# Attention over a K/V cache on one core: V transfers moved to ScalarE's DMA queue, transfers of 512 KB, no limit on bytes outstanding

## The chip, the cores and the metric

One core of a Trainium2 chip. The metric is device time in microseconds (us) of one execution. The kernel before takes 941.17 us (median of 2 runs, 939.9 to 942.44).

## The reference

Two independent blocks, A and B, do the same thing; their outputs are put side by side.

```python
# x: 16 x 64 x 640; k_cache, v_cache: 16 x 32 x 512 x 128; wq: 640 x 4096; wo: 4096 x 640; all bf16
q = (x @ wq).reshape(B, Sq, H, Dh).transpose(0, 2, 1, 3)
scores = einsum("bhqd,bhkd->bhqk", q, k_cache) * Dh ** -0.5
p = softmax(scores)
o = einsum("bhqk,bhkd->bhqd", p, v_cache)
out = o.transpose(0, 2, 1, 3).reshape(B, Sq, H * Dh) @ wo
```

K and V of both blocks are 268 MB, and each byte is used once. With the weights the kernel reads 294.7 MB. There is much to stream, and nearly as much to compute.

## The kernel before

The kernel is a software pipeline that is planned in Python. One *step* is two heads of two batches; there are 256 steps. In each step TensorE (PE) transposes K (KX, 32 small transposes), transposes the softmax rows (TR, 16), projects Q (QP, 10 matmuls), multiplies by V (PV, 16), projects the output (OP, 4) and makes scores (SM, 4). Each matmul instruction also has a weight load, so a step is about 165 PE instructions. ScalarE (ACT) computes exp and copies o; VectorE (DVE) copies transposes out of PSUM; GpSimd normalizes.

K and V lie in rings. A slot holds `G` heads of two batches and is filled by two transfers, one per batch. All loads are issued by SyncE (SP), in an order that the plan finds by counting each transfer's time:

```python
class Cfg:
    G = 2               # heads in a slot; a K or V transfer is G * 128 KB
    CAP = 2100 << 10    # the window: bytes of SP's loads that may be outstanding
    NKB = 10            # slots of the K ring
    NVB = 10            # slots of the V ring
    NXN = 2
...
    for c in range(NCHUNK):
        for kind, ring, n_ring, cons, tb in (("LDK", "kn", cfg.NKB, "KX", 2), ("LDV", "v", cfg.NVB, "PV", 2.5)):
            ready = NEG if c < n_ring else MPC * (c - n_ring + 1) - 1 - OFF[cons]
            need = MPC * c - OFF[cons]
            for j in range(2):
                op = Op("sp", kind, (c, j), [], [(ring, c % n_ring, gi) for gi in range(0, G, 2)],
                        ts=(need, -1), aux=(c, j), dur=cfg.DMA_NS[kind] * G / 2.0)
                loads.append((ready, need, tb + 0.001 * j, op))
    pending = sorted(loads, key=lambda e: (e[1], e[2]))
    ...                               # takes the ready load that is needed first
        progs["sp"].append(e[3])
        t_now += e[3].dur / cfg.SLOT_NS
...
    for op in progs["sp"]:            # the window
        window.append(op)
        done = None
        while sum(size[o.kind] for o in window) > cfg.CAP:
            done = window.pop(0)
        if done is not None:
            op.deps.append(done)      # SP waits until this earlier load has landed
...
        def em_LDKV(e, op):           # (cut)
            if op.kind == "LDV":
                src = blocks[blk][2][2 * bp + j, h0:h0 + G].rearrange("g (p t) d -> p g t d", p=128)
                ins = e.dma_start(v_ring[:, c % NVB, j], src)
            else:
                src = ...             # K, likewise
                ins = e.dma_start(kn_ring[:, c % NKB, j], src)
```

Of the kernel before, what the change touches and what calls it, by code (L numbers as in the profile page):

```python
# [19 lines left out]


class Cfg:
    G = 2
    GW = 4
    CAP = 2100 << 10
    HH = 16
    NKB = 10
    NVB = 10
    NX = 3
    NXN = 2  # L30
    NQ = 2
# [24 lines left out]
        act=("EX0", "EX1", "XE0", "OE0", "OVP0", "ST0"),  # L56
# [26 lines left out]
def build_plan(dims, cfg, stable, counts):  # L83
    NBLK, B, H = dims["NBLK"], dims["B"], dims["H"]
    G, GW = cfg.G, cfg.GW
    HH = min(cfg.HH, H)
    assert H % HH == 0 and HH % G == 0 and G % 2 == 0 and cfg.NR % 2 == 0 and B % 2 == 0
    NHALF = H // HH
# [5 lines left out]
    NMAC = NSTEP // 2  # L94
    NCHUNK = NSTEP // G
    HG = HH // GW
    MPG = HH // 2
    MPP = NBP * MPG
    MPC = G // 2
    MPW = GW // 2  # L100
# [10 lines left out]
    def make_op(eng, kind, sub, k, m):  # L111
        ts = (k, STAGE[kind + str(sub)])

        def mk(idx, reads, writes, aux=None, name=None):
            return Op(eng, name or kind, idx, reads, writes, ts=ts, aux=aux)
# [13 lines left out]
        g = g0 + sub  # L129
        c = g0 // G  # L130
        r = g % cfg.NR
        if kind == "KX":
            return mk(m, [("kn", c % cfg.NKB, g0 % G), ("ident",)], [("KT", 0), ("KT", 1)])
        if kind == "KE":
# [21 lines left out]
        if kind == "PV":  # L156
            return mk(m, [("pT", m % cfg.NT, 0), ("pT", m % cfg.NT, 1), ("v", c % cfg.NVB, g0 % G)], [("B",)])
        if kind == "OE":
# [16 lines left out]
    progs = {e: [] for e in ENGINES}  # L175
    lo = -max(max(OFF.values()), cfg.XLEAD)
    for k in range(lo, NMAC):
        for eng, order in cfg.ENGINE_ORDER.items():
            for name in order:
                kind, sub = name[:-1], int(name[-1])  # L180
                op = make_op(eng, kind, sub, k, k + OFF[kind])
# [15 lines left out]
        progs["dve"].append(Op("dve", "CF", -1, [], [("KT", 0), ("flag",)], ts=(NMAC + 8, 4)))  # L197

    loads = []
    NEG = -10 ** 9  # L200
    for ps_ in range(NPASS):
        buf = ps_ % 2
        for j in range(HG):
            m0 = ps_ * MPP + j * MPW
            for kind, name, cons, tb in (("LDWQ", "wq", "QP", 0), ("LDWO", "wo", "OP", 3)):
                ready = NEG if ps_ < 2 else (ps_ - 1) * MPP - MPG + j * MPW + MPW - 1 - OFF[cons]
                need = m0 - OFF[cons]
                op = Op("sp", kind, (ps_, j), [], [(name, buf, j)], ts=(need, -1), aux=(ps_, j),
                        dur=cfg.DMA_NS[kind])
                loads.append((ready, need, tb, op))  # L210
    for grp in range(NGRP):
        need = MPG * grp - cfg.XLEAD
        op = Op("sp", "LDX", grp, [], [("xn", grp % cfg.NXN)], ts=(need, STAGE["KX0"]), aux=grp,
                dur=cfg.DMA_NS["LDX"])
        loads.append((NEG if grp < cfg.NXN else need - MPG * cfg.NXN, need - 1, 1, op))
    for c in range(NCHUNK):
        for kind, ring, n_ring, cons, tb in (("LDK", "kn", cfg.NKB, "KX", 2), ("LDV", "v", cfg.NVB, "PV", 2.5)):
            ready = NEG if c < n_ring else MPC * (c - n_ring + 1) - 1 - OFF[cons]
            need = MPC * c - OFF[cons]
            for j in range(2):  # L220
                op = Op("sp", kind, (c, j), [], [(ring, c % n_ring, gi) for gi in range(0, G, 2)],
                        ts=(need, -1), aux=(c, j), dur=cfg.DMA_NS[kind] * G / 2.0)
                loads.append((ready, need, tb + 0.001 * j, op))
    pending = sorted(loads, key=lambda e: (e[1], e[2]))
    t_now = min(e[1] for e in loads) - 4.0
    while pending:
# [59 lines left out]
    for op in progs["sp"]:  # L286
# [4 lines that stand above are left out]
# [57 lines left out]
def mha_kernel(nc, blocks, out, cfg=None):  # L348
# [16 lines left out]
    for stable in (False, True):  # L365
        progs, info = build_plan(dims, cfg, stable, counts)
        prune_waits(progs)
        plans.append((progs, info))
    info = plans[0][1]
    NBP, HH, NHALF, NSTEP = info["NBP"], info["HH"], info["NHALF"], info["NSTEP"]  # L370
    NKB, NVB, NX, NXN, NQ, NKT, NP, NPN, NT, NO, NR = (cfg.NKB, cfg.NVB, cfg.NX, cfg.NXN, cfg.NQ, cfg.NKT, cfg.NP,
                                                       cfg.NPN, cfg.NT, cfg.NO, cfg.NR)
# [10 lines left out]
    with contextlib.ExitStack() as es:  # L383
        block = es.enter_context(nc.Block())

        def sb(name, shape, dt):
            return es.enter_context(nc.sbuf_tensor(name, shape, dt))
# [5 lines left out]
        xn_ring = sb("xn_ring", [128, NXN, D], BF16)  # L393
        kn_ring = sb("kn_ring", [128, NKB, 2, G // 2, 8, DH], BF16)
        v_ring = sb("v_ring", [128, NVB, 2, G, 4, DH], BF16)
        ktp_ring = sb("ktp_ring", [128, NKT, 2, 2, SK], BF16)
# [25 lines left out]
        def kt_ps(hs):  # L422
            return ps[:, KT_BANK + hs, :].bitcast(BF16)
# [7 lines left out]
        def rows(r):  # L431
            return slice(64 * r, 64 * r + 64)

        def row_transpose(e, dst, src, r):
            return e.transpose(dst, src, ident[rows(r), rows(r)], tile_position=(64 * r, 0))  # L435

        def em_KX(e, op):
# [3 lines left out]
            for j in range(2):  # L441
                for t8 in range(8):
                    for hs in PAIR:
                        col = 512 * j + 64 * t8
                        ins.append(row_transpose(e, kt_ps(hs)[:, col:col + 64],
                                                 kn_ring[rows(hs), c % NKB, j, hp, t8, :], hs))
            return ins[0], ins[-1]
# [82 lines left out]
        def em_PV(e, op):  # L530
            m = op.idx
            ins = []
            for sub in range(2):
                g = 2 * m + sub
                c, gi = g // G, g % G
                for j in range(2):
                    for t in range(4):
                        col = sub * 128 + 64 * j
                        ins.append(e.matmul(o_ps[:, col:col + 64], v_ring[:, c % NVB, j, gi, t, :],  # L539
                                            pT_ring[:, m % NT, j, sub, t, :], start=(t == 0), stop=(t == 3)))  # L540
# [103 lines left out]
        def em_LDKV(e, op):  # L644
# [3 lines left out]
# [4 lines that stand above are left out]
                src = blocks[blk][1][2 * bp + j, h0:h0 + G].rearrange("(hp hs) (p t) d -> (hs p) hp t d",  # L652
                                                                              hs=2, t=8)
                ins = e.dma_start(kn_ring[:, c % NKB, j], src)
            return ins, ins
# [110 lines left out]
```

## Time and profile before

| | before |
|---|---|
| time, median | 941.17 us |
| steps done by 60 us | 13 |
| steady step, mean of steps 16 to 240 | 3.60 us |
| undisturbed step (10th percentile) | 3.03 us |
| PE gaps that end just after an instruction fetch | 83, together 86 us |

The profiled run took 947.4 us, 0.8% above the fastest of its two timed runs.

The page of the kernel before: span, PE's busy time and instructions, DMA busy tenths and GB/s in 40 slices, two DMA queues (packets, MB, share of 16 engines), and the chain that ended last, by engine.

```profile
span 945.6 us, 48361 instructions
PE 830.7 (88%) x21153; PEld 592.1 (63%) x21153; DVE 669.3 (71%) x1812; ACT 446.6 (47%) x1329; POOL 416.2 (44%) x518
...
DMA  8999999999999999999999999998999999999930
GB/s 293 320 344 354 346 361 356 354 344 355 332 355 336 324 315 318 310 330 325 323 346 363 354 322 330 314 324 278 334 339 324 352 348 302 332 299 326 303 116 12
...
q1 hardware_dynamic: 236544, 294.72, 93.2%
q8 instruction: 170, 2.79, 1.2%
...
PE 77%; issue 10%; DMA 6%; DVE 5%; ACT 1%; SPq 0%; ACTq 0%; DVEq 0%
```

DMA looks saturated by its busy tenths, but the windows view gives 351 GB/s at 60-300 us, then 329 and 321 in the next two stretches of 300 us, so later there is some room. "issue" is time in which PE waited for nothing that the profile shows, and it is 10% of the chain. Two more views say the same. The waits (engine, line, waited for: us in total, times, longest), first PE's and then those of SP's queue:

```profile
PE ps L435 <- issue: 47.1, 44, 2.7
PE ps L539 <- issue: 23.1, 22, 2.1
PE ps L461 <- issue: 11.3, 12, 1.9
```

```profile
SPq L650 <- PE ps L539: 76.5, 112, 3.1
SPq L654 <- PE ps L435: 71.8, 107, 2.4
```

SP waits for PE to free V (L650) and K (L654) slots, so the rings are mostly full. Data is seldom late: all of PE's waits for DMA sum to 15 us, against 81.5 us in the three lines above. What PE lacks shows in the timeline (start, length, engine, line, operation; in brackets the idle time before):

```profile
305.50 0.68 PE L461 MATMUL ps<-xT_ring,wq_sb 128*128 128x128 bf16 x9
307.42 0.23 PE L461 MATMUL ps<-xT_ring,wq_sb 128*128 128x128 bf16 x1 [1.24 <-issue]
307.49 0.63 PE L539 MATMUL ps<-pT_ring,v_ring 128*128 128x64 bf16 x16
```

PE stops between the ninth and the tenth Q matmul. No semaphore is awaited there; the next *instruction* is missing. The DMA records of the trace (queue q8) hold 170 transfers of 16 KB of instructions. One ran from 304.30 to 306.04, and PE went on at 307.42, 1.4 us after it landed. Nearly every gap like this ends 1.2 to 1.7 us after such a transfer, at places in PE's program 251.4 matmul and weight-load instructions apart. With PE's other instructions that is a block of 256. The Trainium skill ("Runtime: NRT & Kernel Launch", Instruction fetch mechanics) describes it: instructions are refilled in 16 KiB blocks of 256, the next while the current one executes. The trace agrees. The skill also calls the cost "mostly hidden", and with 86 us of gaps here the trace does not.

From the records two quantities can be worked out for every fetch:

- **delay**: from PE's start on the block before (taken as the moment of the request) to the start of the fetch's data. An undisturbed block lasts 4.6 us (251.4 instructions at 165.3 a step and 3.03 us a step). The data takes about 1.0 us and PE restarts 1.4 us later, so by this estimate a delay above about 2.2 us stalls PE.
- **backlog**: bytes issued, at the end of their issue instruction, less bytes whose packets have started.

Before, the mean delay is 2.94 us, and the mean backlog at a request is 0.86 MB. The delay depends on which instruction is taken for the start of the block: a check that counted every PE instruction gave means 0.2 us lower.

The first Q projection of the run, and a stretch by the windows view (stretch and its length, busy time of each engine with instruction counts, PE clock, DMA share, GB/s):

```profile
3.97 0.70 ACT L640 ACTIVATE xT_ring<-ps 128x640 bf16<-128x640 bf16 x1 [1.90 <-PE ps L635]
...
6.24 1.25 PE L461 MATMUL ps<-xT_ring,wq_sb 128*128 128x128 bf16 x10 [2.30 <-DMA wq_sb<-in_A_wq_dram]
```

```profile
100.00:850.00 750.00, 670.72 (x17251) 478.34 (x17248) 542.35 (x1472) 363.55 (x1084) 337.54 (x416) 0.98 0.99 332
```

### The profile page before, as it was taken

The numbers are of one execution on the slowest core, as the hardware profiler recorded it, in microseconds if no ns is written. First come the engines' busy times: TensorE is split into PE (matmuls) and PEld (weight loads), VectorE is DVE, ScalarE is ACT, GpSimd is POOL, SyncE is SP. The second block draws the span as 40 slices with busy tenths as digits, with TensorE's granted clock in tenths as the row PEclk, the third lists the DMA queues.
The fourth block names the chain that finished last, engine by engine and source line by source line (L and its number), as shares of the span: only waits on it lengthen the run. The fifth ranks groups of instructions, "written<-read, shape, count | busy, mean of one in ns | idle before, by whom it ended". The sixth has DMA issues, their size and how long they took to land.

```text
span 945.6 us, 48361 instructions
## 1 busy us (share of the span) xinstructions
PE 830.7 (88%) x21153; PEld 592.1 (63%) x21153; DVE 669.3 (71%) x1812; ACT 446.6 (47%) x1329; POOL 416.2 (44%) x518
## 2 busy tenths in 40 slices
PE   6798889888889999989889999998888889898895
PEld 4466666566566666667566666666556566666663
DVE  4477766777567777768677677776667777777785
ACT  3345444454445544544445455554444445445452
POOL 3244444444345444444445444444444444444442
PEclk9899999999999999999999999999999999999999
DMA  8999999999999999999999999998999999999930
GB/s 293 320 344 354 346 361 356 354 344 355 332 355 336 324 315 318 310 330 325 323 346 363 354 322 330 314 324 278 334 339 324 352 348 302 332 299 326 303 116 12
DMA packets 239066, 300.52 MB, mean 318 GB/s; under 512 B 17664, under 2 KB 173312, under 8 KB 238848
## 3 DMA queue, kind: packets, MB, share of 16 engines
q1 hardware_dynamic: 236544, 294.72, 93.2%
q8 instruction: 170, 2.79, 1.2%
q10 hardware_dynamic: 2304, 2.62, 0.8%
q14 instruction: 48, 0.39, 0.1%
HBM read 294.65 MB, written 2.62 MB: 314 GB/s over the span
## 4 chain that ended last, share of the span: by engine, by line
PE 77%; issue 10%; DMA 6%; DVE 5%; ACT 1%; SPq 0%; ACTq 0%; DVEq 0%
PE ps L435 21%; PE ps L461 16%; PE ps L555 14%; PE ps L474 13%; PE ps L539 12%; DMA v_ring<-in_A_v_cache_dram 3%; DVE ktp_ring L451 2%; DVE pT_ring L526 1%; DMA wq_sb<-in_A_wq_dram 1%; DMA wo_sb<-in_A_wo_dram 1%; PE ps L635 1%; DVE out_sb L568 1%; ACT p_ring L495 1%; DMA kn_ring<-in_A_k_cache_dram 1%; DVE qT_ring L467 0%
## 5 line engine op out<-in xcount | busy, mean ns | idle before, releaser
L510 POOL TENSOR_SCALAR pn_ring<-p_ring,recip 128x512 bf16<-128x512 bf16 x512 | 415.6, 840 | 516.0 <-DVE recip L502 516.0
L451 DVE COPY ktp_ring<-ps 128x1024 bf16<-128x1024 bf16 x512 | 345.6, 682 | 158.3 <-PE ps L435 158.2
L495 ACT ACTIVATE p_ring<-ps 128x512 bf16<-128x512 f32 x512 | 300.5, 593 | 49.0 <-DVE out_sb L568 23.0
L544 ACT ACTIVATE oT_ring<-ps 128x256 bf16<-128x256 f32 x256 | 97.9, 383 | 386.3 <-DVE pT_ring L526 385.4
L526 DVE COPY pT_ring<-ps 128x512 bf16<-128x512 bf16 x512 | 193.3, 419 | 85.5 <-PE ps L539 85.1
L435 PEld LDWEIGHTS ps<-ident,kn_ring 64*128 64x128 bf16 x8192 | 138.1, 96 | 125.7 <-issue 105.3
L461 PE MATMUL ps<-xT_ring,wq_sb 128*128 128x128 bf16 x2560 | 193.5, 223 | 13.6 <-issue 11.3
L555 PE MATMUL ps<-wo_sb,oT_ring 128*128 128x512 bf16 (+1 forms) x1024 | 186.6, 305 | 8.2 <-DMA wo_sb<-in_A_wo_dram 6.2
L539 PE MATMUL ps<-pT_ring,v_ring 128*128 128x64 bf16 x4096 | 169.7, 195 | 23.8 <-issue 23.1
L435 PE MATMUL ps<-ident,kn_ring 64*128 64x64 bf16 x8192 | 170.9, 192 | 17.1 <-issue 14.2
L474 PE MATMUL ps<-ktp_ring,qT_ring 128*64 128x512 bf16 x1024 | 165.3, 399 | 3.1 <-issue 1.6
L461 PEld LDWEIGHTS ps<-xT_ring,wq_sb 128*128 128x128 bf16 x2560 | 147.4, 99 | 30.0 <-issue 14.3
L539 PEld LDWEIGHTS ps<-pT_ring,v_ring 128*128 128x128 bf16 x4096 | 149.0, 99 | 27.0 <-issue 25.3
L435 PE MATMUL ps<-ident,pn_ring 64*128 64x64 bf16 x4096 | 108.1, 191 | 38.5 <-issue 32.9
L467 DVE CAST qT_ring<-ps 128x256 bf16<-128x256 f32 x256 | 108.7, 425 | 16.1 <-PE ps L461 7.5
L435 PEld LDWEIGHTS ps<-ident,pn_ring 64*128 64x128 bf16 x4096 | 80.7, 96 | 41.4 <-issue 37.2
L495 ACT ACTIVATION_READ_ACCUMULATOR p_ring<-ps 128x1 f32 x512 | 102.5, 200 | 0.0
L555 PEld LDWEIGHTS ps<-wo_sb,oT_ring 128*128 128x128 bf16 x1024 | 74.1, 99 | 42.7 <-issue 7.0
L474 PEld LDWEIGHTS ps<-ktp_ring,qT_ring 128*64 128x64 bf16 x1024 | 38.3, 108 | 75.7 <-issue 71.6
L502 DVE RECIPROCAL recip<-sums 128x1 f32<-128x1 f32 x512 | 78.6, 153 | 8.8 <-ACT p_ring L495 8.8
L640 ACT ACTIVATE xT_ring<-ps 128x640 bf16<-128x640 bf16 x32 | 22.5, 703 | 55.9 <-PE ps L635 55.9
L635 PE MATMUL ps<-ident,xn_ring 128*128 128x128 bf16 x160 | 15.2, 228 | 4.4 <-DMA xn_ring<-in_A_x_dram 3.2
(16 smaller groups left out, 39.5 us busy)
## 6 DMA issues: line engine op xcount, KB each, us to landing
kn_ring<-in_A_k_cache_dram SPq DMA_DIRECT2D x256, 256.0 KB, 5.4
v_ring<-in_A_v_cache_dram SPq DMA_DIRECT2D x256, 256.0 KB, 5.4
kn_ring<-in_B_k_cache_dram SPq DMA_DIRECT2D x256, 256.0 KB, 5.3
v_ring<-in_B_v_cache_dram SPq DMA_DIRECT2D x256, 256.0 KB, 5.2
wq_sb<-in_A_wq_dram SPq DMA_DIRECT2D x8, 640.0 KB, 5.9
wo_sb<-in_A_wo_dram SPq DMA_DIRECT2D x8, 640.0 KB, 5.7
wq_sb<-in_B_wq_dram SPq DMA_DIRECT2D x8, 640.0 KB, 6.1
wo_sb<-in_B_wo_dram SPq DMA_DIRECT2D x8, 640.0 KB, 6.0
```

The source lines that it names most:

```text
L435: return e.transpose(dst, src, ident[rows(r), rows(r)], tile_position=(64 * r, 0))
L451: ins = e.tensor_copy(ktp_ring[:, m % NKT, hs].rearrange("p j k -> p (j k)"), kt_ps(hs))
L461: ins.append(e.matmul(q_ps[:, sub * 128:(sub + 1) * 128], wq_sb[:, ps_ % 2, kt, hh * DH:(hh + 1) * DH], xT_ring[:, grp % NX, kt, :], start ...
L467: ins = e.tensor_copy(qT_ring[:, op.idx % NQ].rearrange("p s q -> p (s q)"), q_ps)
L474: ins.append(e.matmul(ps[64 * j:64 * j + 64, S_BANK + sub, :], qT_ring[:, m % NQ, sub, 64 * j:64 * j + 64], ktp_ring[:, m % NKT, sub, j, : ...
L495: ins = e.activation(p_ring[:, g % NP, :], ps[:, S_BANK + g % 2, :], ACTF.Exp, scale=scale, accum_out=sums[:, g:g + 1], **kw)
L502: ins = e.reciprocal(recip[:, g % NR:g % NR + 1], sums[:, g:g + 1])
L510: ins = e.tensor_scalar(dst, src, recip[:, r:r + 1], 1.0, ALU.mult, ALU.mult)
L526: ins = e.tensor_copy(pT_ring[:, m % NT, j].rearrange("p s t q -> p (s t q)"), ps[:, A_BANK + j, 0:256].bitcast(BF16))
L539: ins.append(e.matmul(o_ps[:, col:col + 64], v_ring[:, c % NVB, j, gi, t, :], pT_ring[:, m % NT, j, sub, t, :], start=(t == 0), stop=(t == ...
L544: ins = e.activation(oT_ring[:, op.idx % NO].rearrange("p s q -> p (s q)"), o_ps, ACTF.Copy)
L555: ins.append(e.matmul(dst, oT_ring[:, m % NO, sub, :], wo_sb[:, ps_ % 2, hh, c0:c1], start=(hh == 0), stop=(hh == HH - 1)))
```

## The change

The intent is to take V off SP's queue, so that two queues feed the DMA engines, and to use fewer, larger transfers. ScalarE issues a V transfer right after the o copy of the step that freed its slot, so it need not wait. The window goes, and slots double in size while their number halves, so the rings hold as much as before.

```diff
-    G = 2
+    G = 4
-    CAP = 2100 << 10
+    CAP = 64 << 20
-    NKB = 10
-    NVB = 10
+    NKB = 5
+    NVB = 5
...
-                op = Op("sp", kind, (c, j), [], ...
-                loads.append((ready, need, tb + 0.001 * j, op))
+                op = Op("act" if kind == "LDV" else "sp", kind, (c, j), [], ...
+                if kind == "LDV":
+                    v_loads.append(op)
+                else:
+                    loads.append((ready, need, tb + 0.001 * j, op))
+    act = []
+    for op in progs["act"]:
+        while v_loads and v_loads[0].aux[0] < cfg.NVB:
+            act.append(v_loads.pop(0))          # the first fill, ahead of everything
+        act.append(op)
+        while v_loads and op.kind == "OE" and op.idx == MPC * (v_loads[0].aux[0] - cfg.NVB + 1) - 1:
+            act.append(v_loads.pop(0))
+    progs["act"] = act
```

The change's description also names two x buffers; `NXN` was 2 already. So there are four edits in one: size, window, V's queue, and, since V's time no longer counts in SP's plan, SP's order of K and weights.

More of the change, by code (lines that the diff above doesn't have):

```diff
@@ L199, in build_plan @@
     loads = []
+    v_loads = []
     NEG = -10 ** 9
@@ L220, in build_plan @@
             for j in range(2):
-                op = Op("sp", kind, (c, j), [], [(ring, c % n_ring, gi) for gi in range(0, G, 2)],
+                op = Op("act" if kind == "LDV" else "sp", kind, (c, j), [], [(ring, c % n_ring, gi) for gi in range(0, G, 2)],
                         ts=(need, -1), aux=(c, j), dur=cfg.DMA_NS[kind] * G / 2.0)
-                loads.append((ready, need, tb + 0.001 * j, op))
+                if kind == "LDV":
[9 more added lines that the diff above has]
+            act.append(v_loads.pop(0))
+    assert not v_loads
+    progs["act"] = act
     pending = sorted(loads, key=lambda e: (e[1], e[2]))
```

## The prediction

> **What bounds the kernel now.** Neither TensorE's work nor DMA alone. An undisturbed step (two heads, two batches) repeats every 3.03 us in the timeline; 256 steps are 776 us of the 945.6 us span. DMA moves 294.7 MB, 93% of 16 engines busy, but by stretches of time 351 GB/s at 60-300 us and 321-329 after: not saturated later. The chain of waits is 77% PE, 10% "issue" and only 6% DMA, mostly in the first 60 us. In the waits, SP's queue waits 148 us for PE to free K and V slots: the rings are mostly full.
>
> The "issue" time is instruction fetch. In the timeline PE stops inside a group (1.24 us within the Q matmuls at 307.4) where no semaphore is awaited. The DMA records hold 170 instruction transfers of 16 KB, 1.03 us each; the stalls end 1.4 us after one, at places 251.5 PE instructions apart. The Trainium skill, "Runtime: NRT & Kernel Launch", Instruction fetch mechanics, says that instructions come in 16 KiB blocks and the next page is fetched while the current one executes; the trace agrees. A block lasts 4.6 us undisturbed. If its fetch is requested when the previous block begins, data starts 0.95-4.8 us later, median 2.64; later than 2.2 us stalls PE. The delay follows the bytes issued and not yet moved: about 1.0 us + 1.8 us per MB, correlation 0.53, outstanding median 0.9 MB. Gaps over 0.8 us alone are 83 us, nearly all fetches.
>
> **What the change does.** (1) The 2.1 MB window goes: whole rings, 10.5 MB, and two passes' weights can be outstanding. (2) 1 MB is released every two steps per ring instead of 0.5 MB every step; same bytes and capacity. (3) 256 V issues go to ScalarE, 0.34-0.47 us each, sometimes 1-2.4 us on SP now: 0.4 us a step on an engine 47% busy; mostly hidden. (4) SP issues less, which was not the limit. (5) Weights bunch, since SP's order no longer counts V's time.
>
> **On the critical path.** Bursts twice as large raise the mean outstanding by about 0.25 MB (estimate), the fetch delay by 0.45 us per block: 75 us over 165 blocks. Slower PE frees slots more slowly, which lowers the queue again: I keep 35 us. Start: ScalarE issues 5.2 MB of V ahead of its first x copy, and K, x and first weights share bandwidth with V and second-pass weights; fetches wait behind all this. By 60 us I expect 6-9 steps instead of 13: 15 us. Weight bursts and ScalarE issues delaying exp: 5 us. No gain from fuller DMA, since PE is fetch-limited. The skill, "DMA: Bandwidth & Descriptors", Issuing engines are not separate DMA queues, says a second issuing engine saves only issue time; the trace cannot show that yet.
>
> **Prediction: 995 us, 8 in 10 within 940 to 1090.** Faster by over 2%: 0.09; within 2%: 0.17; slower: 0.74.
>
> **What would show it.** Undisturbed step still 3.03 us; PE busy near 830 us; still 170 fetches, but later after their request, and "issue" in the chain above 10%; time to landing of K and V well above 5.4 us; mean GB/s near 300; first Q matmul later than 6.2 us; V issues in ScalarE's idle time, exp seldom waiting.
>
> **What would make it wrong.** If the fetch delay depends on one queue's backlog alone or saturates, splitting could shorten the stalls: then 900-940. If it grows without limit, or ScalarE blocks for microseconds in each issue when the rings are deep: over 1090. If larger transfers run more efficiently, some is given back.

## The result

After takes 1045.89 us (median of 2 runs, 1045.68 to 1046.1), 104.7 us more by the medians. The ratio is 1.111, 95% interval 1.105 to 1.118. Ratios here and below are the mean time of one kernel's fast runs over that of the other's fast runs of the same rounds, so they are not quite the ratio of the medians.

The page after:

```profile
span 1044.4 us, 47398 instructions
PE 839.3 (80%) x21153; PEld 598.6 (57%) x21153; DVE 672.0 (64%) x1812; ACT 448.8 (43%) x1329; POOL 415.8 (40%) x518
...
DMA  9999887889998889888899888897888888888850
GB/s 322 364 363 360 285 270 252 283 278 294 352 364 276 286 291 303 288 281 268 290 366 313 286 296 287 288 300 275 290 289 273 271 295 281 279 294 290 281 169 14
...
q1 hardware_dynamic: 93184, 160.45, 44.4%
q10 hardware_dynamic: 137472, 136.86, 40.6%
q8 instruction: 170, 2.79, 1.1%
...
PE 69%; issue 16%; DVE 7%; ACTq 4%; ACT 2%; DMA 1%; SPq 0%; DVEq 0%
```

V is on a queue of its own now (q10). PE's work is the same 21153 matmuls, and the fetches are the same 170. "issue" went from 10% to 16% of the chain, and ScalarE's queue (ACTq) came in with 4%. PE's waits and SP's:

```profile
PE ps L448 <- issue: 75.3, 53, 3.1
...
PE ps L552 <- issue: 36.3, 27, 2.4
...
PE ps L474 <- issue: 27.6, 18, 2.5
```

```profile
SPq L667 <- PE ps L448: 597.5, 119, 9.0
```

The three PE waits for "issue" (K and P transposes, PV, Q) were 47.1, 23.1 and 11.3 us. SP waits 597.5 us for PE to free K slots (L667; before, 71.8 us on L654), and PE's own waits for DMA sum to 11 us (before, 15), so data is even less late than before. A stall as shown of before; the fetch behind it ran from 326.05 to 327.08:

```profile
325.09 0.37 PE L448 MATMUL ps<-ident,pn_ring 64*128 64x64 bf16 x14
...
328.51 0.20 PE L448 MATMUL ps<-ident,pn_ring 64*128 64x64 bf16 x2 [3.05 <-issue]
328.65 0.73 PE L474 MATMUL ps<-xT_ring,wq_sb 128*128 128x128 bf16 x10
```

The start, and the same stretch as before in the windows view:

```profile
0.80 23.49 ACTq L663 DMA_DIRECT2D v_ring<-in_A_v_cache_dram  x10
...
9.45 7.88 SPq L667 DMA_DIRECT2D kn_ring<-in_A_k_cache_dram  x2
...
25.61 0.70 ACT L653 ACTIVATE xT_ring<-ps 128x640 bf16<-128x640 bf16 x1
26.45 1.22 PE L474 MATMUL ps<-xT_ring,wq_sb 128*128 128x128 bf16 x10 [21.66 <-ACT xT_ring L653]
```

```profile
100.00:850.00 750.00, 624.58 (x15864) 445.92 (x15860) 500.00 (x1353) 336.47 (x998) 311.10 (x384) 0.98 0.88 294
```

The ten V issues ahead of everything took 23.49 us on ScalarE, an average of 2.3 us each, because an issue now *blocks*. Counting packets, ScalarE's queue had 1.9 to 2.4 MB outstanding when one of these ten was held for over 2 us; SP's held issues of the first 66 us began with 2.0 to 3.2 MB on its queue. Later some issues took 1.5 to 2.1 us with only 0.2 to 1.1 MB on their queue, which is not explained. The x copy stands behind these issues, so the first Q projection starts at 26.45 us instead of 6.24 us.

Where the time went, from the start of Q copies in the two traces:

| stretch | before | after | difference |
|---|---|---|---|
| until step 16 | 71.8 us | 98.7 us | +26.9 |
| steps 16 to 240 | 805.5 us (3.60 a step) | 873.4 us (3.90 a step) | +67.9 |
| rest, to PE's last matmul | 62.2 us | 66.0 us | +3.8 |

From 60 us to the end PE's gaps that end with a fetch (those over 0.2 us) went from 86 to 149 us. Within steps 16 to 240 they went from 83 to 137 us, which is 54 of the 67.9 us. All other gaps there grew by some 5 us, and PE's busy time grew by 9 us (719.5 to 728.5), for which no run gives the cause.

The mean delay rose from 2.94 to 3.35 us and the mean backlog at a request from 0.86 to 1.12 MB. After has a larger spread of backlog, so the dependence shows better: delay = 1.3 us + 1.8 us per MB, correlation 0.83 (before 0.27 over its narrower range; the prediction, with its own choice of the request, found 0.53). Moving a whole MB at after's 294 GB/s takes 3.4 us, so by this estimate a fetch waits for about half of what is outstanding, and not for all of it. Fitted with a slope for each queue, it is 1.78 us per MB of SP's backlog and 1.82 of ScalarE's: here a fetch waits behind both queues alike. In small_v_on_act (below) the same fit gives about 1.0 and 2.3, so equal slopes are not a rule.

The spread matters more than the mean. Sampled over 100 to 850 us, the mean backlog rose only from 0.89 to 1.02 MB, but its 10th and 90th percentiles went from 0.55 and 1.22 to 0.19 and 1.76 MB. PE loses time only when a delay is above its 2.2 us or so, and low delays give nothing back.

### The profile page after: what moved, and what is told of

Read it like the earlier page. It is cut to its first block, busy times and chain, and to the rows that moved or that the text cites. A ratio compares the mean times of both kernels' runs of the same rounds, so it can differ in the third digit from the quotient of the medians.

```text
span 1044.4 us, 47398 instructions
## 1 busy us (share of the span) xinstructions
PE 839.3 (80%) x21153; PEld 598.6 (57%) x21153; DVE 672.0 (64%) x1812; ACT 448.8 (43%) x1329; POOL 415.8 (40%) x518
## 3 DMA queue, kind: packets, MB, share of 16 engines
HBM read 294.65 MB, written 2.62 MB: 285 GB/s over the span
## 4 chain that ended last, share of the span: by engine, by line
PE 69%; issue 16%; DVE 7%; ACTq 4%; ACT 2%; DMA 1%; SPq 0%; DVEq 0%
PE ps L448 19%; PE ps L474 15%; PE ps L487 12%; PE ps L568 12%; PE ps L552 11%; ACTq L663 4%; DVE ktp_ring L464 2%; DVE pT_ring L539 2%; ACT p_ring L508 2%; DMA kn_ring<-in_A_k_cache_dram 1%; PE ps L648 1%; DVE qT_ring L480 1%; DVE out_sb L581 1%; DVE recip L515 1%; ACT oT_ring L557 0%
## 5 line engine op out<-in xcount | busy, mean ns | idle before, releaser
L474 PE MATMUL ps<-xT_ring,wq_sb 128*128 128x128 bf16 x2560 | 196.0, 224 | 49.3 <-issue 27.6
L487 PE MATMUL ps<-ktp_ring,qT_ring 128*64 128x512 bf16 x1024 | 168.4, 398 | 11.0 <-issue 6.7
L448 PEld LDWEIGHTS ps<-ident,pn_ring 64*128 64x128 bf16 x4096 | 81.5, 96 | 58.9 <-issue 54.6
L487 PEld LDWEIGHTS ps<-ktp_ring,qT_ring 128*64 128x64 bf16 x1024 | 40.6, 108 | 88.9 <-issue 75.4
```

What stands on the lines that cost most here:

```text
L448: return e.transpose(dst, src, ident[rows(r), rows(r)], tile_position=(64 * r, 0))
L474: ins.append(e.matmul(q_ps[:, sub * 128:(sub + 1) * 128], wq_sb[:, ps_ % 2, kt, hh * DH:(hh + 1) * DH], xT_ring[:, grp % NX, kt, :], start ...
L487: ins.append(e.matmul(ps[64 * j:64 * j + 64, S_BANK + sub, :], qT_ring[:, m % NQ, sub, 64 * j:64 * j + 64], ktp_ring[:, m % NKT, sub, j, : ...
```

## The experiments

**Theory A:** the instruction fetch waits behind the data outstanding on every queue; larger and unlimited transfers raise what is outstanding. **Rival B:** V issues hold up exp and the o copy on ScalarE. The start is a third part, with causes of its own. Twelve kernels ran. The table gives all; "stalls" are PE gaps over 0.2 us that end with a fetch, over the whole run; "backlog" is at the request. The two quarter-V runs have no backlog, since its count assumes full transfers.

| run | median us | ratio (95%) | step 16 at | steady step | stalls us | delay us | backlog MB |
|---|---|---|---|---|---|---|---|
| before | 941.2 | 1 | 71.8 | 3.60 | 86 | 2.94 | 0.86 |
| after | 1045.9 | 1.111 (1.105-1.118) | 98.7 | 3.90 | 153 | 3.35 | 1.12 |
| small_no_window | 957.6 | 1.018 (1.011-1.024) | 74.9 | 3.63 | 98 | 2.93 | 0.95 |
| big_window | 988.9 | 1.048 (1.041-1.054) | 79.1 | 3.75 | 120 | 3.19 | 0.96 |
| v_on_sp | 1010.9 | 1.071 (1.065-1.078) | 75.1 | 3.84 | 133 | 3.26 | 1.12 |
| big_release_small_transfers | 976.5 | 1.033 (1.025-1.041) | 75.3 | 3.70 | 116 | 3.08 | 0.93 |
| small_v_on_act | 963.4 | 1.024 (1.019-1.030) | 97.6 | 3.55 | 76 | 2.85 | 0.92 |
| small_v_on_act_late | 963.8 | 1.023 (1.018-1.028) | 99.0 | 3.54 | 75 | 2.87 | 0.91 |
| small_v_on_act_late_order | 960.9 | 1.024 (1.020-1.029) | 87.2 | 3.58 | 85 | 2.94 | 0.91 |
| after_late_order | 1038.5 | 1.105 (1.099-1.111) | 88.0 | 3.90 | 134 | 3.36 | 1.16 |
| small_v_on_act_late_order_window | 990.5 | 1.051 (1.045-1.058) | 95.6 | 3.65 | 83 | 2.96 | 0.88 |
| v_128k | 989.3 | 1.052 (1.047-1.057) | 73.0 | 3.80 | 55 | 2.62 | 0.60 |
| before_quarter_v (wrong result) | 866.3 | 0.919 (0.913-0.925) | 70.0 | 3.25 | 27 | 1.89 | - |
| after_quarter_v (wrong result) | 915.5 | 0.971 (0.965-0.978) | 93.9 | 3.37 | 55 | 2.31 | - |

The fast runs of one kernel scatter by up to 1.5%, while steps, stalls and delays are of one profiled run each. Differences of a per cent between those are not leaned on. Which gaps count as a fetch's is a choice of how soon after the fetch they must end; in v_128k, with many other waits, it moves the sum between 47 and 68 us, elsewhere by 10 us at most.

One cost is in none of these columns. The traces record the granted TensorE clock. In the fourteen traces, between 60 and 800 us and in the stretches of 3.41 us by which that record changes, PE was busy for less than 45% of a stretch 114 times; 113 times the next stretch ran at half clock. (39 more half-clock stretches followed busier ones.) A long fetch stall can thus cost more than its own length. In steps 16 to 240, before spent 31 us at half clock, after 34, v_on_sp 71 and after_late_order 72. At half clock at most half of that time is lost, so some 20 us of v_on_sp's and after_late_order's loss against before may come by the clock (estimate). It is not a chance of single traces: the mean granted clock of the fast runs was 0.983 to 0.986 for before, 0.969 for big_window, 0.963 for v_on_sp and 0.959 for after_late_order. No run takes this part away alone.

### v_on_sp: V back on SP's queue

```diff
 # against before
-    G = 2
+    G = 4
-    CAP = 2100 << 10
+    CAP = 64 << 20
-    NKB = 10
-    NVB = 10
+    NKB = 5
+    NVB = 5
```

> All transfers on SP's queue again, but still 512 KB each and without the 2.1 MB window. Theory A (the instruction fetch waits behind every byte outstanding, whichever queue it is on; what raised the backlog is the size and the missing window): the steady step stays near the 3.90 us of after (3.8-4.0), mean fetch delay near 3.35 us; only the start comes back (first Q matmul near 7.5 us, some 15-25 us), so about 1015-1030 us. Rival B (V issues on ScalarE hold up exp and the o copy): step falls back to 3.6-3.7 us and the time to 945-970 us.

Measured: 1010.9 us, step 3.84 us, delay 3.26 us, backlog 1.12 MB, start as before (step 16 at 75.1). Theory A's numbers, within its range. With not one V issue on ScalarE, two thirds of the loss is still there (69 of 104.7 us). The other third, 35 us from here to after, is in the traces 23.6 us of start and 12.8 us of steady steps (224 steps, 0.057 us each). That third is what Rival B and the changed order of SP's loads have to share. The split is rough: between the same steps the fetch stalls rose by 18 us (119 to 137), while v_on_sp lost more to the half clock. PE's waits in v_on_sp show the same waits for instructions without V on ScalarE (before: 47.1, 23.1 and 11.3 us):

```profile
PE ps L435 <- issue: 66.5, 51, 2.8
PE ps L539 <- issue: 30.8, 24, 2.4
PE ps L461 <- issue: 23.6, 16, 2.8
```

### small_no_window: only the window removed

```diff
-    CAP = 2100 << 10
+    CAP = 64 << 20
```

> Before with one edit: no window. Theory A with the missing window as the cause: backlog at the fetch request rises from 0.86 MB towards 1.1 MB, fetch delay from 2.94 to 3.3 us or more, step to 3.8-3.9 us, 980-1010 us. Theory A with the transfer size as the cause (bursts of 1 MB): step stays at 3.6-3.7 us, 941-960 us. Rival B: no change at all, 941 us.

Measured: 957.6 us, ratio 1.018. The window is worth about 16 us and not the bulk. Time and step (3.63 us) lie in the ranges given for "size as the cause". The mean delay hardly moved (2.93 us), but its 90th percentile rose from 3.97 to 4.31 us.

### big_window: only the size

```diff
-    G = 2
+    G = 4
-    NKB = 10
-    NVB = 10
+    NKB = 5
+    NVB = 5
```

> Before with one edit: 512 KB transfers, window of 2.1 MB kept, all on SP. If size alone does it: step 3.8-3.9 us, 985-1010 us. If the missing window does it: backlog stays bounded, 941-960 us. Rival B: 941 us.

Measured: 988.9 us, the low side of what size was expected to do. The step of 3.75 us missed the range of 3.8-3.9; part of the time is a slower start (step 16 at 79.1 us). Size raises the time by 4.8% under the window and by about 5.2% without it (1.071 over 1.018). So size is the largest single part of the change.

### big_release_small_transfers: what about size?

Slots of four heads are still freed as one, so 1 MB is still released at once, but each 512 KB transfer is cut into two of 256 KB, issued back to back.

```diff
 # against v_on_sp (sources and destinations cut accordingly; a semaphore for each piece)
-            for j in range(2):
-                op = Op("sp", kind, (c, j), [], [(ring, c % n_ring, gi) for gi in range(0, G, 2)], ...
+            for half in reversed(range(G // 2)):
+                for j in range(2):
+                    op = Op("sp", kind, (c, j, half), [], [(ring, c % n_ring, 2 * half)], ...
```

> One queue, no window, slots of four heads freed together as in v_on_sp, but each 512 KB transfer is cut into two of 256 KB issued back to back, so the burst of 1 MB per release stays. Theory A1 (what hurts is the burst: how much is released at once): as v_on_sp, step 3.8-3.9 us, 1000-1015 us. Theory A2 (what hurts is the single transfer: a longer run of one DMA on each engine ahead of the fetch): as small_no_window, step 3.6-3.65 us, 950-965 us.

Measured: 976.5 us, between the two and in neither range. Of the 53 us between small_no_window and v_on_sp (another chip, whose runs of before differ by under 1 us in the median), releasing at once gives 19 us, and the single transfer's size 34 us. Both matter, the latter more. Why the cut helps is not settled. More issues take longer, which by itself spreads the burst (the backlog at requests is 0.93 MB and not 1.12), and a shorter transfer could also let the fetch in sooner. No run separates these two.

### small_v_on_act: V by ScalarE, at 256 KB

```diff
 # against after
-    G = 4
+    G = 2
-    NKB = 5
-    NVB = 5
+    NKB = 10
+    NVB = 10
```

> After with 256 KB transfers and rings of 10: V on ScalarE's queue, no window, 512 V issues there instead of 256. If size is the cause: step falls to 3.6-3.7 us, and 975-990 us with the slow start kept. If the missing window is the cause: step stays 3.85-3.95, 1030-1050 us. Rival B (ScalarE issues cost): twice the number of issues, so the step rises above 3.95 us and the time above 1060 us.

Measured: 963.4 us, below every range: the steady step fell to 3.55 us, which is lower than small_no_window's 3.63. Doubling the V issues on ScalarE did not raise the step, so Rival B falls for the steady part. What is lost against before is the start (step 16 at 97.6 us). In this trace exp waited 44.7 us in all for ScalarE's issues between 100 and 850 us, yet PE's gaps without a fetch after 60 us sum to only 7 us: exp has slack. The fetch stalls fell too, from small_no_window's 98 to 76 us at about the same backlog, so at 256 KB a second queue may even have helped the fetch; at 512 KB it did not (133 to 153). No run separates the reason.

### before_quarter_v and after_quarter_v: is it really the data?

Wrong results: after the first ring fill a V transfer brings 32 of 128 partitions. Instructions, issues and waits stay.

```diff
-                ins = e.dma_start(v_ring[:, c % NVB, j], src)
+                n = 128 if c < NVB else 32
+                ins = e.dma_start(v_ring[0:n, c % NVB, j], src[0:n])
```

> Wrong result on purpose: after the first ring fill V transfers bring 32 of 128 partitions, a quarter of the bytes; all waits, issues and instructions as before. Theory A (stalls are fetches behind outstanding data): backlog about 0.5 MB, fetch delay mostly under 2.2 us, stalls under 20 us, step 3.05-3.2 us, 820-860 us. If the stalls had another cause (PE's own, or a fixed fetch time): step stays near 3.5-3.6 us, about 930 us.

> The same cut in the kernel after the change. 256 V issues still on ScalarE. Theory A: the step falls to 3.1-3.3 us, and what is left of the difference to before_quarter_v is the start (some 20-25 us): 845-890 us. Rival B (ScalarE issues cost in the steady state): the difference to before_quarter_v stays 50 us or more outside the start.

Measured: 866.3 us, just above the range (as are its step and its stalls), and 915.5 us, above it. Steady steps are 3.25 and 3.37 us with a median of 3.03 us in both: most steps are now undisturbed. Stalls fell from 86 to 27 us and from 153 to 55 us, with PE's instructions untouched. PE's waits in before_quarter_v:

```profile
PE ps L435 <- issue: 11.3, 18, 1.4
PE ps L539 <- issue: 8.1, 10, 2.4
...
PE ps L461 <- issue: 3.0, 5, 1.1
```

That settles that the data traffic, and not PE or a fixed fetch time, makes the stalls. It cannot tell bytes that wait from bytes that move; v_128k below, which moves all bytes with less backlog and has fewer stalls, speaks for those that wait. The remaining difference of the two traces is 23.9 us of start and 27.8 us of steady steps; after 60 us the fetch stalls differ by 23 to 26 us and the other gaps by 2 to 4 us. The expectation for after missed, perhaps because K's bursts of 1 MB alone still stall PE; no run tests that.

### small_v_on_act_late, small_v_on_act_late_order, after_late_order: the start

First, the first fill of V is issued by steps and not ahead of everything. Then also SP's order is planned with V's time counted again. Last, both in the changed kernel itself.

```diff
 # late
-        while v_loads and v_loads[0].aux[0] < cfg.NVB:
-            act.append(v_loads.pop(0))
         act.append(op)
+        # first two steps' V after the first x copy, the V of step m+2 after exp of step m;
+        # then up to four issues after an o copy, each once its slot is free
 # order
-                else:
-                    loads.append((ready, need, tb + 0.001 * j, op))
+                loads.append((ready, need, tb + 0.001 * j, op))
...
-        progs["sp"].append(e[3])
+        if e[3].kind != "LDV":
+            progs["sp"].append(e[3])
```

> V on ScalarE's queue at 256 KB, no window, but the first ring fill is issued by steps (two chunks after the first x copy, then one per exp pair) instead of 20 transfers ahead of everything. If the slow start of small_v_on_act is the blocked ScalarE queue: first Q matmul near 7.5 us instead of 30.7, 13 or more steps by 60 us, about 20 us off 963 us: 935-948 us, so level with before. If it was only moved (DMA-bound fill): still 955-965 us.

Measured: the first Q copy came at 7.2 us instead of 30.6, and the time did not move: 963.8 us, step 16 at 99.0. The loss was only moved.

> As small_v_on_act_late (V by ScalarE, 256 KB, first fill by steps, no window), and SP's order of K and weights as before, by counting V's time again though V is not on SP. If the lost start (step 16 at 98.8 us instead of 71.8) is the second pass's weights put ahead of K: step 16 near 72-76 us and 935-945 us, level with before or slightly faster. If the start is lost to two queues sharing the bandwidth: still 955-965 us.

Measured: step 16 at 87.2 us, 12 us of the start back in the trace, but the time is 960.9 us, within the scatter of 963.8. The expected 935-945 us did not come.

> The changed kernel (512 KB, no window, V by ScalarE) with the same two repairs of its start. If the start is the weights' order and the blocked first issues: step 16 near 75-80 us, the steady step unchanged at 3.85-3.9 us, 1015-1027 us instead of 1046. If the steady step were also hurt by the bunched weights, below 1010 us.

Measured: 1038.5 us, less of a gain than expected (7 us, the two intervals overlap), steady step unchanged at 3.90 us (with fewer fetch stalls but twice the time at half clock). Step 16 is at 88.0 us and not 75. The timeline of this run shows what is left:

```profile
43.47 9.97 ACTq L671 DMA_DIRECT2D v_ring<-in_A_v_cache_dram  x3
53.48 0.60 ACT L516 ACTIVATE p_ring<-ps 128x512 bf16<-128x512 f32 x1 [10.05 <-issue]
...
54.22 0.64 PE L495 MATMUL ps<-ktp_ring,qT_ring 128*64 128x512 bf16 x2 [7.81 <-ACT p_ring L516]
...
55.39 6.13 ACTq L671 DMA_DIRECT2D v_ring<-in_A_v_cache_dram  x2
```

Three V issues hold ScalarE for 9.97 us, exp comes after them, and PE waits 7.81 us for exp. So Rival B is right about the start, where the queues are full: there an issue takes as long as data needs to drain, and ScalarE has work that PE needs. How much of the rest of the start is due to two queues drawing data out of the order of need is open.

### small_v_on_act_late_order_window and v_128k: towards a faster version

The first puts a window of 1050 KB on SP (K and weights) in small_v_on_act_late_order:

```diff
-    CAP = 64 << 20
+    CAP = 1050 << 10
```

> As small_v_on_act_late_order with a window of 1050 KB on SP's half of the bytes (half of before's 2100 KB). If bounding the backlog helps two queues as it helped one (16 us of 958): another 5-15 us, 922-937 us, faster than before. If V's unbounded half sets the peaks: no change against small_v_on_act_late_order.

Measured: 990.5 us, slower than both alternatives expected. PE now waits for K:

```profile
PE ps L456 <- DMA kn_ring<-in_A_k_cache_dram: 26.1, 7, 7.7
...
PE ps L456 <- DMA kn_ring<-in_B_k_cache_dram: 6.8, 4, 3.7
```

Without the window the same two waits summed to 6.9 us. The window held SP back while ScalarE's queue was not held. Half the window for SP's share of the bytes was too little. One of its six runs was slow and is left out.

The second cuts before's V transfers to one head, 128 KB, four per step:

```diff
 # against before (sources, destinations and semaphores cut accordingly)
-                op = Op("sp", kind, (c, j), [], ...
+                for h in ((0, 1) if kind == "LDV" else (0,)):
+                    op = Op("sp", kind, (c, j, h), [], ...
```

> Before with V cut further: four transfers of 128 KB (one head) instead of two of 256 KB per step, window and everything else the same, about 2.6 us of issue per step on SP. If smaller transfers go on helping: delay below 2.8 us, step 3.5-3.57 us, 920-935 us. If the gain ends at 256 KB or SP's issue time becomes the limit: 941-965 us.

Measured: 989.3 us. The fetch stalls did what theory A says: 55 us, delay 2.62 us, backlog 0.60 MB. But a new limit came in, as the second alternative said, and harder than its range. In this run's chain and PE's waits:

```profile
SPq 35%; PE 27%; DMA 27%; issue 6%; DVE 3%; ACT 1%; ACTq 0%; DVEq 0%
```

```profile
PE ps L436 <- DMA kn_ring<-in_A_k_cache_dram: 30.5, 33, 3.3
PE ps L436 <- DMA kn_ring<-in_B_k_cache_dram: 29.5, 30, 3.5
PE ps L540 <- DMA v_ring<-in_A_v_cache_dram: 14.7, 20, 1.3
```

K and V issues took SP 804 us in all (1536 issues, 0.52 us on average), which is 3.14 us per step against an undisturbed step of 3.03 us. SP could not issue fast enough, and data came late. It no longer waited for free slots (before, 76.5 us on V alone):

```profile
SPq L651 <- PE ps L540: 16.4, 36, 1.6
```

Before's 256 KB lies between two losses, fetch stalls above and issue time below. No version here beats the kernel before.

## Why the prediction was right or wrong

The direction, the cause and the range were right: 1045.9 us lies in 940 to 1090. The central 995 us was low, since it added 54 us and 104.7 came.

- **Fetch-limited, not DMA-limited: right.** before_quarter_v takes 76 us off by taking bytes away (0.919 of before), with PE's instructions unchanged. Alone this would fit a DMA limit too; that PE waited 81.5 us for instructions and 15 us for data, with the rings mostly full, tells the two apart.
- **Backlog +0.25 MB, delay +0.45 us per block: right.** Measured +0.26 MB and +0.41 us.
- **The mis-sized term is the damping.** "Slower PE frees slots more slowly, which lowers the queue again: I keep 35 us" of 75. Measured are 67.9 us in the steady part, 54 of them fetch stalls, and 62 us of added fetch stalls from 60 us to the end, against the 75 before damping. The rate did fall, from 332 to 294 GB/s, but the backlog at a request still stood 0.26 MB higher. A likely reason is that a burst of 1 MB stays 1 MB however far apart the bursts come. That is argued and not tested, and it is not all: big_window has the same burst and a backlog of 0.96 MB.
- **The start: right in kind, too small.** "15 us" was 26.9 us. The 9 steps by 60 us were in the forecast range of 6 to 9. The prediction gave blocking issues only as a risk, but the ten first V issues held ScalarE for 23.49 us with some 2 MB outstanding on its queue, and "whole rings, 10.5 MB" were never outstanding (at most 4.9 MB in after's trace). Blocking is not the whole loss: unblocking the first issues alone gained nothing (small_v_on_act_late).
- **V issues "mostly hidden": right in the main for the steady part, wrong for the start.** small_v_on_act doubled them and its step fell; in after_late_order's start three issues held exp for 10 us.
- **The burst of release as the cause: half right.** big_release_small_transfers gives it 19 us of 53; the size of the single transfer, which the prediction did not name, gives 34.
- **Signs.** Undisturbed step 3.03 us, 170 fetches, "issue" 16%, 288 GB/s in the mean and a later first Q matmul came as written; PE was busy 839 us. Exp waited 41 us for ScalarE's issues, 33 times, which is not quite "seldom". Time to landing rose less than "well above 5.4 us": K 7.3 and 6.8 us, V only 6.0 and 5.1.

By edit, as ratios to before: the window alone +1.8%, then slots released by four heads +1.5%, then whole 512 KB transfers +3.8%, then V on ScalarE +4.0%, of which two thirds is start. The order of the edits is a choice; at 256 KB, V on ScalarE costs only 0.6% more than the window's removal, with intervals that overlap.

## What to carry to other kernels

When an engine runs tens of thousands of unrolled instructions beside a heavy stream of data, its instruction fetches may wait behind that data, as here. Look for gaps inside groups where no semaphore is awaited, and compare them with the instruction queue's transfers. If they match, try fewer bytes outstanding, more evenly spread, with transfers as small as the issuing engine can afford. Letting more be outstanding while the rings were full bought nothing here and cost 1.8% (small_no_window). Before moving transfers to the queue of an engine that also computes, check how long one issue takes when the queue is full: everything behind it waits.

## What the Trainium skill lacked or had wrong

- "Runtime: NRT & Kernel Launch", Instruction fetch mechanics, calls crossing a block "mostly hidden". With data streaming at 332 GB/s before and 294 after (100 to 850 us), PE's fetch gaps were 86 us of 946 before and 153 us of 1044 after.
- "DMA: Bandwidth & Descriptors", Queues, rings and completion order, says that each DMA engine takes turns between queues packet by packet. If that were all, the fetch's delay should not grow with a deep backlog; it grew by 1.8 us per MB, for either data queue (1.78 and 1.82 in after), to some 5.5 us in after's steady part. The page does not say how the wait of a small transfer on a queue of its own grows with what other queues hold.
- The same page's Rules for kernel authors advise 1 MiB or more per DMA for bandwidth. Here 512 KB in place of 256 KB, with four heads freed at once, cost 4.8% (big_window): the instruction fetches beside it waited longer, and their stalls went from 86 to 120 us.
- The same page, Issuing engines are not separate DMA queues, says a second issuing engine saves only issue time. For bandwidth no run contradicts it. It lacks that an issue can block its engine when about 2 MB are outstanding on its queue (in the first fill of after 1.9 to 2.4 MB on ScalarE's and 2.0 to 3.2 MB on SP's; 1.6 to 1.9 MB on ScalarE's in after_late_order): 23.49 us for ten issues, 9.97 us for three.
